# Attention and a gated FFN on one core: batch 0 with a mask product, single PSUM banks and split weight loads

## The chip, the cores and the metric

The kernel runs on one core of a Trainium2 chip. The core has a tensor engine (PE) with its weight loads (PEld), a vector engine (DVE), a scalar engine (ACT), GpSimd (POOL) and SyncE (SP), which here only issues DMAs. The metric is the device time of one execution in microseconds (us); lower is better. The median of 8 runs of the kernel before is 380.19 us (379.68 to 382.72).

## The reference

```python
B, H, S, D = 8, 8, 576, 64
scores = q @ k.T / 8
cum = cumsum(max(s, 0))                       # per head, along the sequence
scores = scores + min(-(cum[i] - cum[j]), 0)  # the bias
scores = where(j > i, -1e9, scores)           # causal mask
attn = softmax(scores) @ v
x = attn, heads side by side                  # 4608 tokens x 512
g = x @ w_gate                                # 512 x 1536
out = (silu(g) * (x @ w_val)) @ w_out         # 1536 x 512
```

All inputs are float32; the kernel computes its matrix products in bfloat16 with float32 sums.

## The kernel before

**Attention.** There are 64 heads: 8 batches of 8. Four heads make one half batch `hb` (16 of them). Q and K of a half batch are transposed into `KQ[hb % 2][r]`, where 64 partitions hold a head's channels and the other 64 hold four rows with the cumulated bias (`aug`, line 192) and zeros, so that one matmul gives score plus bias. `HL` holds these rows; it comes from `s` by a chain on DVE (lines 236 to 242). A head's scores are made transposed, keys on partitions, in four pieces (`CHUNKS`, line 56): 512 columns on the diagonal, 512, 512 and 64. ACT takes the exponential of a piece out of PSUM into `pt`, and POOL's `affine_select` sets the entries above the diagonal to zero (lines 391 and 396). `av_piece` multiplies with V and a column of ones, `av_out` divides by the sum on DVE, `x_pe` transposes the result on PE into `XT`.

**FFN.** A tile is 512 tokens; there are 9. For each of 12 blocks of 128 FFN columns, `gate_value` makes the gate product (4 matmuls of 128x512, line 626), tanh on ACT, a product on DVE, the value product (line 641) and a second product on DVE. `down_plain` or `down_seven` then multiplies with w_out.

**Order.** The program order of each engine is written out by hand. Batch 0 runs alone, in `first_batch`. After it, the FFN of tile `tt` is interleaved with the attention of batch `tt` + 1: `ffn_items` yields after each product, and `pump` advances `attn_items` in proportion. `hook` places the transposes of half batch 2 and some casts among the first items. Half batches 2 to 4 are transposed on PE (`prep_one`, `PREP_AT`), later ones through DRAM by DMA.

**PSUM.** In batch 0 it is cut into two wide tiles of two banks (1024 columns) and four single banks; `second_psum` makes eight single banks of it afterwards. In batch 0 a head's four pieces are written in pairs into a wide tile, so that ACT runs two exponentials per head, of 1024 and 576 columns. A bank is taken with `take` (the one released longest ago) and given back with `give`.

**Queues.** SP issues the loads of q, k, v and the bias rows of half batches 0, 2 and 3 (`SP4`); POOL issues the weights (`w_load`, which casts to bfloat16 on the way), the bias rows of half batch 1 (`GP4`) and the stores. Each engine runs its instructions in order, so an instruction that waits holds up all behind it. In `first_batch` the first gate and value tiles (768 columns each) are issued after head 1's scores, the second ones after heads 4 and 5, w_out after head 7. V of batch 0 is cast by POOL (three chunks, after head 2) and DVE (two chunks, after head 1). All eight heads' values come after head 6's scores:

```python
tail = {
    6: ("a0", "a1"),
    7: ("a2", "a3", "a4", "x0", "a5", "x1", "a6", "a7", "x2", "w6", "x3", "w8"),
}
```

where a is `av_piece` and `av_out` of a head, x is `x_pe` of a pair of heads and w are matmuls whose result nobody reads.

The softmax here doesn't subtract the row's maximum and nothing guards it: scores larger than these inputs give would overflow.

## Time and profile before

| | us |
|---|---|
| median of 8 runs | 380.19 |
| the profiled execution | 379.68 |
| its span | 377.9 |
| first score matmul of batch 0 | 11.21 |
| end of batch 0's last exponential | 27.03 |
| first gate product | 31.68 |
| first value product | 32.81 |

The span is the time from the first to the last instruction that the profile records; the execution's own time is 1.8 us longer. In the page, the busy share of each engine over the span is followed by 40 slices of 9.45 us, each a digit in tenths. PEclk is the share of the PE clock that was granted. The chain is followed back from the last instruction to what released each step. A row of the timeline has its start, its busy time, engine, line, operation, the tiles written and read with their shapes, and the number of instructions merged in it; in brackets stands how long the engine was idle before it and what ended that. Where one row has several shapes, the first is printed. A row of a table by stretches has the stretch, its length, each engine's busy time with its instructions, the granted clock, the mean busy share of the 16 DMA engines and GB/s. A semaphore record tells when a DMA's data landed.

### The profile page before, as it was taken

To read this page: it belongs to the slowest core of one execution; us is meant where nothing else is said; L and a number is where in the kernel's file an instruction comes from. 1 tells how busy PE (TensorE), PEld (TensorE's weight loads), DVE (VectorE), ACT (ScalarE), POOL (GpSimd) and SP (SyncE) were. 2 spreads that over 40 slices of the span, in tenths; PEclk is the share of its full clock that TensorE was granted. 3 is DMA by queue.
4 is the path that set the end of the run, shared out by engine and by line. 5 is a ranking of instruction groups with operands and counts; after the bars stand their busy time and mean duration, and the time that the engine had idled before them with its cause. 6 is when DMAs were issued, how large, how long until landed. Compare 5 with 4: busy or idle time off the path is not lost.

```text
span 377.9 us, 8674 instructions
## 1 busy us (share of the span) xinstructions
PE 361.5 (96%) x3246; PEld 229.5 (61%) x3246; DVE 290.2 (77%) x577; ACT 242.4 (64%) x459; POOL 206.5 (55%) x326
## 2 busy tenths in 40 slices
PE   3679999999999999999999999999999999999996
PEld 3566556655555546865586558655875575466465
DVE  7766787457895899769975998589958876985984
ACT  8686788677976877578766885697365523323321
POOL 7684357545374646595559556875675426224320
PEclk9899999999999999999999999999999999999999
DMA  7999999997498997498669775996323133001103
GB/s 241 198 251 262 199 260 265 343 263 169 159 170 280 214 289 202 124 291 212 166 203 287 195 161 162 231 215 144 52 71 111 24 28 128 0 2 69 43 2 111
DMA packets 100730, 64.22 MB, mean 170 GB/s; under 512 B 81889, under 2 KB 85825, under 8 KB 100689
## 3 DMA queue, kind: packets, MB, share of 16 engines
q1 hardware_dynamic: 91248, 46.15, 50.3%
q0 software_dynamic: 9440, 17.53, 17.8%
q8 instruction: 25, 0.41, 0.5%
q14 instruction: 17, 0.13, 0.1%
HBM read 37.90 MB, written 19.86 MB: 153 GB/s over the span
## 4 chain that ended last, share of the span: by engine, by line
PE 85%; DVE 6%; DMA 5%; ACT 2%; issue 1%; DVEq 0%; ACTq 0%; SPq 0%
PE bank L626 22%; PE bank L641 22%; PE bank L711 17%; PE bank L375 9%; PE bank L413 6%; PE bank L670 5%; DMA pk<-ks 3%; PE wide L375 2%; DVE pp L633 1%; ACT pt L388 1%; DVE kq L326 1%; DVE ht L649 1%; PE one L413 1%; DMA kq<-HL 1%; DMA s_sb<-in_s_dram 1%
## 5 line engine op out<-in xcount | busy, mean ns | idle before, releaser
L388 ACT ACTIVATE pt<-bank 128x512 bf16<-128x512 f32 x224 | 106.7, 507 | 26.4 <-PE bank L375 18.1
L626 PE MATMUL bank<-XT,wg 128*128 128x512 bf16 x432 | 110.9, 379 | 0.7 <-DVE pp L633 0.2
L641 PE MATMUL bank<-XT,wv 128*128 128x512 bf16 x432 | 110.9, 379 | 0.0
L631 ACT ACTIVATE th<-bank 128x512 bf16<-128x512 f32 x108 | 64.7, 599 | 58.9 <-PE bank L626 54.7
L633 DVE SCALAR_TENSOR_TENSOR pp<-th,bank 128x512 bf16<-128x512 bf16 x108 | 73.7, 683 | 23.7 <-ACT th L631 23.2
L649 DVE SCALAR_TENSOR_TENSOR ht<-pp,bank 128x512 bf16<-128x512 bf16 x108 | 74.2, 687 | 10.4
L658 POOL TENSOR_TENSOR ht<-ht 128x512 bf16<-128x512 bf16 x35 | 40.4, 1154 | 53.0 <-DVE su L656 53.0
L375 PE MATMUL bank<-kq 128*128 128x128 bf16 (+4 forms) x504 | 67.5, 240 | 0.2 <-DVE ht L649 0.2
L375 PEld LDWEIGHTS <-kq 128*128 128x128 bf16 x576 | 46.3, 99 | 33.7 <-issue 5.0
L641 PEld LDWEIGHTS <-wv 128*128 128x128 bf16 x432 | 38.3, 98 | 35.3
L626 PEld LDWEIGHTS <-wg 128*128 128x128 bf16 x432 | 38.4, 98 | 35.2 <-issue 1.1
L391 POOL TENSOR_SCALAR_AFFINE_SELECT pt<-pt 128x512 bf16<-128x512 bf16 x64 | 42.1, 657 | 30.6 <-ACT pt L388 30.0
L413 PEld LDWEIGHTS <-pt 128*128 128x128 bf16 x960 | 41.0, 98 | 16.6 <-issue 0.7
L413 PE MATMUL bank<-vt,pt 128*128 128x65 bf16 x840 | 41.8, 194 | 0.5 <-DVE ot L430 0.5
L447 POOL DMA_DIRECT2D xs<-ot x24 | 21.7, 906 | 28.2 <-DVE ot L430 28.2
L711 PEld LDWEIGHTS <-ht 128*128 128x128 bf16 x336 | 31.2, 98 | 4.3
L197 POOL DMA_DIRECT2D kq<-HL x52 | 31.3, 605 | 0.1
L430 DVE TENSOR_TENSOR ot<-bank,rc 128x320 bf16<-128x320 f32 x56 | 27.5, 492 | 1.9
L396 POOL TENSOR_SCALAR_AFFINE_SELECT pt<-pt 128x64 bf16<-128x64 bf16 x64 | 17.2, 269 | 18.5 <-ACT pt L388 18.3
L711 PEld LDWEIGHTS <-su 128*128 128x128 bf16 x252 | 23.5, 98 | 3.3
L670 PE MATMUL bank<-wo,ht 128*128 128x512 bf16 x96 | 24.7, 379 | 0.0
L776 POOL TENSOR_TENSOR ysb<-ysb 128x512 f32<-128x512 f32 x12 | 15.2, 1270 | 15.3 <-DVE ysb L770 15.3
(96 smaller groups left out, 396.1 us busy)
## 6 DMA issues: line engine op xcount, KB each, us to landing
rawk<-in_k_dram SPq DMA_DIRECT2D x15, 576.0 KB
rawq<-in_q_dram SPq DMA_DIRECT2D x15, 576.0 KB
rawv<-in_v_dram SPq DMA_DIRECT2D x32, 256.0 KB
out_dram<-ysb POOLq DMA_DIRECT2D x32, 256.0 KB, 3.7
xs<-ot POOLq DMA_DIRECT2D x24, 160.0 KB, 4.0
ks<-ck SPq DMA_DIRECT2D x11, 288.0 KB
qs<-cq SPq DMA_DIRECT2D x11, 288.0 KB
wg<-in_moe_w_gate_dram POOLq DMA_DIRECT2D x2, 768.0 KB, 12.5
```

What stands on the lines that cost most here:

```text
L375: nc.tensor.matmul(sc[:, o : o + w], T[:, 1, e * S + 128 * tj : e * S + 128 * (tj + 1)], T[:, 0, e * S + lo : e * S + hi], start=True, sto ...
L388: nc.scalar.activation(pt[:, c0 : c0 + W], sc[:, 0:W], AF.Exp, scale=0.125)
L391: nc.gpsimd.affine_select(pt[:, 1088:1600], pt[:, 1088:1600], pattern=[[0, 4], [1, 128]], compare_op=ALU.is_ge, fill=zreg, base=0, channel ...
L413: nc.tensor.matmul(av[:, bi * (D + 1) : (bi + 1) * (D + 1)], pt[:, c0 : c0 + 128], VT[b % 2][:, tj, h, :], start=(tj == 0), stop=(tj == bi),)
L626: nc.tensor.matmul(pg, WG[j][:, c, f0 : f0 + 128], xt[:, c, :], start=(c == 0), stop=(c == 3),)
L631: nc.scalar.activation(th, pg, AF.Tanh, scale=0.5)
L633: nc.vector.scalar_tensor_tensor(pp, in0=th, scalar=1.0, in1=pg, op0=ALU.add, op1=ALU.mult)
L641: nc.tensor.matmul(pv, WV[j][:, c, f0 : f0 + 128], xt[:, c, :], start=(c == 0), stop=(c == 3),)
L649: nc.vector.scalar_tensor_tensor(hp[:, 2 * k2 : 2 * k2 + 2, :].rearrange("p a n -> p (a n)"), in0=pp, scalar=0.5, in1=pv, op0=ALU.mult, op ...
L658: (nc.vector if ft == NFT - 1 else nc.gpsimd).tensor_sub(hp[:, 1:3, :], hp[:, 1:4:2, :], hp[:, 0:3:2, :])
L670: nc.tensor.matmul(py, hps[ft // 2][:, 2 * (ft % 2) + half, c0 : c0 + 128], WO[ft // WKO][:, ft % WKO, :], start=(ft == 0), stop=(ft == NF ...
L711: nc.tensor.matmul(ps, lhs(p), rhs(p), start=(first and p == 0), stop=(last and p == NP - 1), skip_group_check=True,)
```

## The change

Batch 0 is written anew, and some places in the later schedule move.

- The wide PSUM tiles are gone; eight single banks serve the whole kernel. One is set aside (`spare`) for matmuls that nobody reads (`keep_warm`): 32 at the start and twice 10 between the first transposes.
- In batch 0, POOL's selects are gone. For the two diagonal pieces a matmul of the identity with a tile `lower` (zero, or -32768 above the diagonal) is put into the bank first, and the scores are added to it. ACT runs four exponentials per head.
- The transposes of half batch 1 are split: k's after head 0, q's after head 1, with the copies of heads 4 and 5 at once and those of heads 6 and 7 after head 3.
- V of batch 0 is cast by POOL alone. The first gate and value tiles are loaded in halves of 384 columns: gate's first half ahead of the bias rows of half batch 1, value's first half after four of the five V casts, the other two after the fifth. The second tiles follow after head 3, with the casts of half batch 2 between them; w_out moves to the fifth FFN item.
- The values of heads 0 and 1 come before head 6's scores, those of 2 and 3 before head 7's, the rest behind. The last `x_pe` copies on DVE. The gate products of the first two blocks run over three of the four head pairs (`begun`) before the FFN starts, and the FFN adds the fourth.
- Seven `pt` buffers instead of eight in batch 0. Later: the second copy of a `prep_one` waits for the next item (`seconds`); the bias rows of half batch 4, some casts, splits and transposes move by a step or more.

```diff
-    PTP = {0: first, "bufs": 8}
+    PTP = {0: first, "bufs": 7}
+    lower = first.tile([128, 512], BF16)
...
-        first_psum = ExitStack()
-        psa = first_psum.enter_context(tc.tile_pool(name="psa", bufs=1, space=PSUM))
-        bank = {}
-        for i in range(2):
-            bank["w", i] = psa.tile([128, 1024], FP32, name=f"wide{i}")
-        for i in range(4):
-            bank["s", i] = psa.tile([128, 512], FP32, name=f"one{i}")
-        released = {key: i - 8 for i, key in enumerate(bank)}
+        psb = ctx.enter_context(tc.tile_pool(name="psb", bufs=1, space=PSUM))
+        bank = {i: psb.tile([128, 512], FP32, name=f"bank{i}") for i in range(8)}
+        released = {i: i - 8 for i in bank}
...
+        nc.gpsimd.memset(lower, 0.0)
+        nc.gpsimd.affine_select(
+            lower, lower, pattern=[[0, 4], [1, 128]],
+            compare_op=ALU.is_ge, fill=nc.gpsimd.to_reg(MASKED), base=0, channel_multiplier=-1,
+        )
...
-        init_vt(0)
-        init_vt(1)
...
+            masked = bh < H
             if ci == 0:
                 pts[bh] = PTP[0].tile(
-                [128, PTW], BF16, tag="pt", bufs=PTP["bufs"], name="pt"
-            )
+                    [128, PTW], BF16, tag="pt", bufs=PTP["bufs"], name="pt"
+                )
             pt = pts[bh]
             r, e = divmod(hh, 2)
             T = KQ[hb % 2][r]
-            if pair:
-                if ci % 2 == 0:
-                    bs = take("w")
-                    scs[bh] = bs
-                else:
-                    bs = scs[bh]
-                base = (512, 0, 0, 512)[ci]
-            else:
-                bs = take()
-                base = 0
-            o = base
+            bs = take()
             n = sum(hi - lo for _, lo, hi in CHUNKS[ci])
-            sc = view(bs, 1024 if pair else 512)
+            sc = view(bs, n)
+            masked_here = masked and ci in (0, 3)
+            if masked_here:
+                nc.tensor.matmul(
+                    sc, ident, lower[:, 0:n], start=True, stop=False, skip_group_check=True
+                )
+            o = 0
             for (tj, lo, hi) in CHUNKS[ci]:
                 w = hi - lo
                 nc.tensor.matmul(
                     sc[:, o : o + w],
                     T[:, 1, e * S + 128 * tj : e * S + 128 * (tj + 1)],
                     T[:, 0, e * S + lo : e * S + hi],
-                    start=True,
+                    start=not masked_here,
                     stop=True,
+                    skip_group_check=masked_here,
                 )
                 o += w
-            if not pair or ci % 2 == 1:
-                if pair:
-                    c0, W = ((576, 1024), (0, 576))[ci // 2]
-                else:
-                    c0, W = CHUNK_PT[ci], n
-                nc.scalar.activation(pt[:, c0 : c0 + W], sc[:, 0:W], AF.Exp, scale=0.125)
-                give(bs)
-            if ci == (1 if pair else 0):
+            c0 = CHUNK_PT[ci]
+            nc.scalar.activation(pt[:, c0 : c0 + n], sc, AF.Exp, scale=0.125)
+            give(bs)
+            if masked:
+                return
+            if ci == 0:
...
-                first = 1 if hb < NPE + 2 else 0
+                first = 1 if hb < NPE + 3 else 0
...
-                if (step, ci) == ((1, 1) if late else (0, 2)):
+                if (step, ci) == ((1, 3) if late else (0, 2)):
                     cast_one(hb, "k", nc.scalar)
-                if (step, ci) == ((2, 1) if late else (1, 2)):
+                if (step, ci) == ((2, 2) if late else (1, 2)):
                     cast_one(hb, "q", nc.scalar)
...
+        V4_AT = {(0, 0): 0, (1, 0): 1, (2, 0): 2, (3, 0): 3, (3, 2): 4}
+
         def side_v(h, step, ci):
             bn = h // 2 + 1
-            if 2 <= bn < B and h % 2 == 1 and (step, ci) in V_AT:
-                cast_v(bn, V_AT[step, ci], nc.scalar if bn > 2 else nc.gpsimd)
+            at = V4_AT if bn == 4 else V_AT
+            if 2 <= bn < B and h % 2 == 1 and (step, ci) in at:
+                cast_v(bn, at[step, ci], nc.scalar if bn > 2 else nc.gpsimd)
...
-            for r in range(2):
-                pe_out(hb, nm, g, r, nc.scalar if nm == "k" else nc.vector)
+            eng = nc.scalar if nm == "k" else nc.vector
+            pe_out(hb, nm, g, 0, eng)
+            seconds.append(lambda: pe_out(hb, nm, g, 1, eng))
...
-            2: {(0, 3): 0, (1, 3): 1, (2, 1): 2, (2, 3): 3},
+            2: {(1, 1): 0, (1, 3): 1, (2, 1): 2, (2, 3): 3},
...
-                    if step == 0 and 3 < h + 1 < NPE:
+                    if step == 2 and 3 < h + 1 < NPE:
...
+        begun = {}
+
+        def products(kind, ft, xt, cs=range(4)):
+            j, f0 = divmod(ft * 128, WCH)
+            w = (WG if kind == "g" else WV)[j]
+            if (kind, ft) in begun:
+                bs, c0 = begun.pop((kind, ft))
+                cs = range(c0, 4)
+            else:
+                bs = take()
+            for c in cs:
+                nc.tensor.matmul(
+                    view(bs, TT), w[:, c, f0 : f0 + 128], xt[:, c, :],
+                    start=(c == 0), stop=(c == 3),
+                )
+            if cs[-1] < 3:
+                begun[kind, ft] = bs, cs[-1] + 1
+            return bs
...
+        spare = take()
+
+        def keep_warm(n):
+            for _ in range(n):
+                nc.tensor.matmul(view(spare, 128), ident, ident, start=True, stop=True)
+
+        def row_half(nm, r, eng):
+            for g in range(2):
+                pe_transpose_half(0, nm, g, r)
+            for g in range(2):
+                pe_out(0, nm, g, r, eng)
+
+        def half_batch(nm):
+            for g in range(2):
+                pe_transpose(1, nm, g)
+                pe_out(1, nm, g, 0, nc.vector)
+
+        def scores(h):
+            for ci in range(4):
+                score_piece(h, ci)
+
+        def values(*hs):
+            for h in hs:
+                av_piece(h, range(NCH))
+                av_out(h)
+
+        keep_warm(32)
         cast_half(0, "k", 0, nc.scalar)
         cast_half(0, "q", 0, nc.scalar)
         aug(0, SP4)
         load_v(0, range(5))
         load_qk(2)
+        row_half("k", 0, nc.scalar)
+        row_half("q", 0, nc.vector)
+        cast_half(0, "k", 1, nc.scalar)
+        cast_half(0, "q", 1, nc.gpsimd)
+        w_load("g", 0, 0)
+        aug(1, GP4)
+        init_vt(0)
+        keep_warm(10)
+        row_half("k", 1, nc.scalar)
+        row_half("q", 1, nc.vector)
+        keep_warm(10)
+        cast_one(1, "k", nc.vector)
+        cast_one(1, "q", nc.vector)
+        for c in range(4):
+            cast_v(0, c, nc.gpsimd)
+        w_load("v", 0, 0)
+        cast_v(0, 4, nc.gpsimd)
+        w_load("g", 0, 1)
+        w_load("v", 0, 1)
+        scores(0)
+        half_batch("k")
+        scores(1)
+        half_batch("q")
+        scores(2)
+        scores(3)
         for nm in ("k", "q"):
             for g in range(2):
-                pe_transpose_half(0, nm, g, 0)
-        pe_out(0, "k", 0, 0, nc.scalar)
-        pe_out(0, "k", 1, 0, nc.scalar)
-        pe_out(0, "q", 0, 0, nc.vector)
-        pe_out(0, "q", 1, 0, nc.vector)
-        cast_half(0, "k", 1, nc.scalar)
-        cast_half(0, "q", 1, nc.gpsimd)
-        aug(1, GP4)
-        for nm, eng in (("k", nc.scalar), ("q", nc.vector)):
-            for g in range(2):
-                pe_transpose_half(0, nm, g, 1)
-                pe_out(0, nm, g, 1, eng)
-        cast_one(1, "k", nc.vector)
-        cast_one(1, "q", nc.vector)
-
-        def keep_warm(n):
-            bs = take()
-            for _ in range(n):
-                nc.tensor.matmul(
-                    view(bs, 128), ident, ident, start=True, stop=True
-                )
-            give(bs)
-
-        def first_batch():
-            wq = {1: (("g", 0), ("v", 0)), 4: (("g", 1),), 5: (("v", 1),)}
-            tail = {
-                6: ("a0", "a1"),
-                7: ("a2", "a3", "a4", "x0", "a5", "x1", "a6", "a7", "x2", "w6", "x3", "w8"),
-            }
-            for h in range(H):
-                for ci in range(4):
-                    score_piece(h, ci)
-                for w in wq.get(h, ()):
-                    w_load(*w)
-                if h == 1:
-                    order = [(nm, g) for g in range(2) for nm in ("k", "q")]
-                    for nm, g in order:
-                        pe_transpose(1, nm, g)
-                    for r in range(2):
-                        for nm, g in order:
-                            pe_out(1, nm, g, r, nc.vector)
-                    for c in range(3, 5):
-                        cast_v(0, c, nc.vector)
-                if h == 2:
-                    for c in range(3):
-                        cast_v(0, c, nc.gpsimd)
-                if h == 3:
-                    aug(2, SP4)
-                if h == 7:
-                    aug(3, SP4)
-                    load_qk(3)
-                    load_v(1, range(5))
-                    load_qk(4)
-                    cast_one(2, "k", nc.gpsimd)
-                    cast_one(2, "q", nc.gpsimd)
-                    load_qk(5)
-                    w_load("o", 0)
-                    w_load("o", 1)
-                for what in tail.get(h, ()):
-                    i = int(what[1:])
-                    if what[0] == "a":
-                        av_piece(i, range(NCH))
-                        av_out(i)
-                    elif what[0] == "x":
-                        x_pe(i, nc.scalar)
-                    else:
-                        keep_warm(i)
-
-        first_batch()
-        second_psum()
+                pe_out(1, nm, g, 1, nc.vector)
+        aug(2, SP4)
+        w_load("g", 1)
+        cast_one(2, "k", nc.gpsimd)
+        cast_one(2, "q", nc.gpsimd)
+        w_load("v", 1)
+        scores(4)
+        scores(5)
+        values(0, 1)
+        scores(6)
+        values(2, 3)
+        scores(7)
+        aug(3, SP4)
+        load_qk(3)
+        load_v(1, range(5))
+        load_qk(4)
+        load_qk(5)
+        init_vt(1)
+        values(4, 5)
+        x_pe(0, nc.scalar)
+        values(6, 7)
+        x_pe(1, nc.scalar)
+        x_pe(2, nc.scalar)
+        x_pe(3, nc.vector)
+        for ft in range(2):
+            products("g", ft, XT[:, :, 0:TT], range(3))
+        give(spare)
...
+            5: [lambda: w_load("o", 0), lambda: w_load("o", 1)],
...
+                while seconds:
+                    seconds.pop(0)()
```

## The prediction

> **What bounds the kernel now.** First the page: PE's row and its slices, then the chain.
>
> ```profile
> PE 361.5 (96%) x3246; PEld 229.5 (61%) x3246; DVE 290.2 (77%) x577; ACT 242.4 (64%) x459; POOL 206.5 (55%) x326
> ...
> PE   3679999999999999999999999999999999999996
> ...
> PEclk9899999999999999999999999999999999999999
> DMA  7999999997498997498669775996323133001103
> ...
> PE 85%; DVE 6%; DMA 5%; ACT 2%; issue 1%; DVEq 0%; ACTq 0%; SPq 0%
> ```
>
> PE is full from the fourth slice to the end; only the first three (28 us) have room. The DMA digits say that the engines moving data are full up to about 94 us. In the chain of waits nearly every 128x512 group of four takes 0.86 us, 0.216 each. Setting each matmul's start-to-start time against its columns at that rate leaves 3.5 us of PE stall after 31.68 us, 2.0 of it near 41, 49 and 136 us. So the end is **the time of the first gate product, plus a fixed load of PE, plus stalls**. The timeline shows what sets that start:
>
> ```profile
> 11.21 0.86 PE L375 MATMUL wide<-kq 128*128 128x128 bf16 x9 [1.22 <-DMA kq<-HL]
> 16.90 4.99 ACT L388 ACTIVATE pt<-wide 128x1024 bf16<-128x1024 f32 x6 [1.38 <-PE wide L375]
> 27.14 0.24 POOL L396 TENSOR_SCALAR_AFFINE_SELECT pt<-pt 128x64 bf16<-128x64 bf16 x1
> 29.87 0.49 DVE L430 TENSOR_TENSOR ot<-one,rc 128x320 bf16<-128x320 f32 x1
> 30.99 0.64 ACT L468 COPY XT<-one 128x576 bf16<-128x576 bf16 x1 [0.52 <-PE one L463]
> 31.68 1.02 PE L626 MATMUL bank<-XT,wg 128*128 128x512 bf16 x4 [0.17 <-ACT XT L468]
> ```
>
> Head 0 waits for its bias rows, ACT's exponentials then run to 27.03 (two gaps, three with the start), POOL masks the last head, and values, normalisation, transpose and copy follow one another to 31.68.
>
> **The change, part by part.**
>
> *Start to 11.2 us.* The bias rows' path (s, DVE's scan, HL, SP's DMAs) has the same instructions. Warm-up matmuls fill PE while it waits: 32 x 0.107 = 3.4 us from 1.4 us end before the first cast at 5.35. Nothing. The ten after q's first half may push k's second half by 0.5 us; ACT has 1.6 us free before 11.86. Nothing. POOL's mask tile costs about 0.5 (a 64x512 memset took 0.52) plus 0.63 (a 128x512 select), against 1.8 us of v-tile memsets moved away; POOL idled 1.3 us there anyway.
>
> *Exponentials.* Wide: heads start 1.715 apart in steady state. Single banks: the full head at 39.41 has its three 512s 0.48 apart, and a 64 adds 0.11: 1.55 per head. First exponential at 11.6 (after 512 columns, not 1024) instead of 11.86; eight heads end at 11.6 + 8 x 1.55 = 24.0. Only three banks stay free while half_batch holds four: refilling one costs PE 0.44 plus about 0.4 of latency, against 0.6 to 1.0 of exponentials beside it; I take 0.4 us off: **24.4** if nothing else stops ACT (before 27.03).
>
> *Mask by a product.* 0.216 + 0.03 us of PE per head, 2.0 in all, beside 0.67 of scores: 0.92 under ACT's 1.55, so hidden; 2.0 us if PE were the bound. POOL loses 8 x (0.655 + 0.259) = 7.3 us. On the path it removes the last POOL step, 0.35 us.
>
> *V casts, all on POOL.* The semaphore records put V's five chunks at 14.4, 15.5, 16.7, 18.1 and 19.2. POOL's casts were 0.56 apart; c3 ends at 18.9, the load of the first value half is issued (0.8), c4 ends at **20.4**. Behind this wait on POOL: both later half loads, then g1 and batch 1's casts. PE wants these values after head 5's scores, near 20, and heads 6 and 7 stand behind them in PE's order.
>
> *The gate half beside the bias rows.* Its issue (0.8) comes ahead of aug(1) on POOL, so those rows land by 15 to 16 instead of 13.9; head 4 wants them at 17.8. Here a rule speaks against the change: the Trainium skill, "DMA: Bandwidth & Descriptors", section "Issuing engines are not separate DMA queues", says that DMAs of all engines run on the same 16 and interleave. The rows:
>
> ```profile
> 8.00:10.00 2.00, 1.88 (x18) 1.71 (x18) 1.38 (x3) 1.17 (x3) 1.76 (x3) 1.00 0.97 383
> 10.00:12.00 2.00, 0.79 (x9) 0.65 (x10) 1.97 (x4) 0.39 (x2) 1.44 (x3) 1.00 0.23 60
> 12.00:22.00 10.00, 6.75 (x63) 5.46 (x61) 7.35 (x12) 7.68 (x10) 7.18 (x14) 0.83 1.14 260
> 22.00:30.00 8.00, 7.24 (x162) 6.34 (x161) 4.66 (x16) 6.14 (x9) 6.92 (x13) 1.00 1.16 212
> ```
>
> Last but one column: DMA share. There is a hole at 10 to 12. aug(1), issued at 8.90 on the same queue, had its first packet 1.34 us later. If the half (512 packets, each half of a 135 ns packet, on 16 engines: 2.2 us) starts at 10.4, most lies in the hole, and V comes 0.3 later or less. By the rule, with the whole half interleaved with V, V lands 1.9 later: c4 at 22.0 and the start 1.6 later. I take the hole, since these rows show the engines free when the half arrives, and keep 22.0 for the range.
>
> *Clock.* The skill's "TensorE: Matmul & The Clock Gate", section "What's actually happening", says that an idle window of about 3.4 us halves the clock. The page's 8 in PEclk is that: 0.5 from 13.0 to 16.4 in the clock record, with batch 0's 18 transposes 0.107 apart. The section "PE-mode transpose" says that transposes don't count as busy, which would leave the clock low in the new order too: 0.9 us more for the same 18. By the warm-up matmuls it stays full. It falls beside ACT's work either way, so on the path I take 0.2.
>
> *The tail.* With c4 at 20.4, PE finishes the two heads' values at about 21.1, head 6's exponentials run 21.6 to 23.1, values 2 and 3, head 7's exponentials 23.6 to 25.1, its values end at 25.9. DVE's eight normalisations at 0.67 from 20.8 give 26.2 or, behind the last values, 26.7. Transpose to 27.2, and six of the gate products (1.3 us) start at once while DVE copies (0.46). Start at 27.2 to 28.8 (c4 at 22.0); with 0.4 for banks I take **28.2, or 3.5 earlier**. The price if the six didn't cover the copy is 0.6.
>
> *After the start.* Total PE work is unchanged. `seconds` takes one of two 0.8 us copies out of DVE's burst at 40 to 49 us: 0 to 1.0 of stall back, I take 0.3; the stall at 136 I leave. w_out's loads move behind the value tile (POOL 1.7 us more at about +5; they landed at 46.7 and 51.7, first wanted at 61.7). aug for heads 16 to 19 moves two heads later, to about 62: rows under load landed 5.4 to 6.8 after issue, wanted near 71. Casts of k5 and q5 go later on ACT, V4's earlier, PREP_AT and `first` by one step: each moves work of 0.5 to 1.2 us among free spaces of ACT and DVE; nothing, or 0.3 either way.
>
> *What is late next* is DMA. Batch 1's V shares the engines with weights:
>
> ```profile
> 53.86 1.17 POOL L183 CAST vt<-rawv 128x512 bf16<-128x512 f32 x2 [0.50 <-DMA rawv<-in_v_dram]
> 55.39 0.35 PE L413 MATMUL bank<-vt,pt 128*128 128x65 bf16 x6
> ```
>
> PE first uses it at 55.39. c2 was cast by 53.37 and c4 by 55.03, wanted at about 56.6 (head 0's scores began on its own bias row at 11.16 while head 1's landed at 11.5, so waits are by region): slack 1.5 to 2.0. The filled hole brings all later transfers 1.0 to 1.9 forward, so PE may come 2.8 to 3.3 earlier before it waits here. That cuts 3.5 + 0.3 to **3.0**. Against the profiled execution: span 377.9 - 3.0 = 374.9, time 379.68 - 3.0 = 376.7; the median shown is 0.5 above that execution, so 380.19 - 3.0 = 377.2.
>
> **Rivals.**
> *V of batch 1 takes the gain.* If the half's packets find no hole, or smaller packets cost more, later transfers come at best 0 to 0.5 earlier, and PE stops at batch 1's values with 0.5 to 1.5 left in place of 3.0: 379.2. For it: DMA share 1.14 from 30 to 54 and that 0.50 wait. Against it: the slack above.
> *The V cast of batch 0 sets the start.* c4 at 23 or later (V delayed and POOL waiting on each chunk): each us goes straight to the start, about 30.5 to 31.5; 379.8.
> *Slower: the first value half.* It is issued only after c3, at 19.8 to 21.4, against 16.6 for the whole tile before. Before, the gate tile took 4.7 us to its first packet and 10.6 to land, the value tile 13.6. Half the bytes with nothing ahead: 4.7 + 2.9 = 7.6, landing at 27.4 to 29.0; the first value product comes at about 29.7, so it decides nothing up to 30. With the old 13.6 from 20.8 it lands at 34.4, while the old kernel ran that product at 32.8: 1.6 slower, 381.8. It decides beyond 32.8.
> *The change doesn't do what it says*: a mask product kept out of the cover of ACT shows as at most 2.0 us of PE and turns 3.0 into 1.0; this is inside the range.
>
> **How the numbers follow.** Main case 0.58 (375.8 to 378.6), V of batch 1 0.20, V cast 0.07, slower 0.15. No change that a measurement can tell is 0.3%, 1.14 us, so 379.05 to 381.33. Faster: 0.57 of the main case and 0.06 of the first rival, 0.63; slower: 0.15 and a little for unknown stalls, 0.16; same 0.21. The range takes the main case, both rivals of little gain, and part of the slower one: 375.6 to 381.0.
>
> **What would show it.** The first gate product at 27 to 29; exponentials 1.55 apart per head up to head 5, then a wait of PE for V's cast of at most 1 us; DMA share at 10 to 12 well above 0.23; no POOL select before batch 1; PEclk without an 8; PE stall after the start still under 4 us. Wrong if the first value product waits for its weights, if heads are over 1.7 apart, or if PE stops at batch 1's values by more than 1 us.

## The result, and the profile after

The changed kernel takes 383.69 us (median of 11 runs, 381.13 to 386.75). The kernel before, run beside it, takes 380.48 us (32 runs, 378.92 to 382.72). The ratio is 1.0088, 95% interval [1.0066, 1.0109]: **0.9% slower**, where 0.8% faster was forecast. The profiled execution took 383.09 us (before: 379.68), its span is 381.4 us (377.9).

The page of the changed kernel: PE's busy row, PE's slices, the clock, the DMA slices, and the shares of the chain.

```profile
PE 366.3 (96%) x3300; PEld 232.0 (61%) x3300; DVE 291.1 (76%) x576; ACT 242.7 (64%) x474; POOL 204.2 (54%) x316
...
PE   7889989989999999999999999999999999999995
...
PEclk9999999999999999999999999999999999999999
DMA  7999999999577986698869765995123013002103
...
PE 73%; DMA 12%; DVE 6%; SPq 4%; POOL 2%; issue 1%; ACT 1%; DVEq 0%; ACTq 0%
```

PE is fuller at the left edge (first three slices 7, 8, 8 instead of 3, 6, 7), but those at 48 to 57 and at 76 to 86 us are 8. The clock row has no 8 any more. In the chain, DMA rose from 5% to 12%, SyncE's queue (SPq) from 0% to 4%, and PE fell from 85% to 73%: the end now hangs more often on data that had not come. The start, in the timeline (rows of ACT, PE and POOL):

```profile
11.58 10.18 ACT L368 ACTIVATE pt<-bank 128x512 bf16<-128x512 f32 x24 [1.59 <-PE bank L358]
...
20.99 0.31 PE L395 MATMUL bank<-vt,pt 128*128 128x65 bf16 x5 [0.79 <-POOL vt L168]
...
21.66 0.62 POOL L168 CAST vt<-rawv 64x512 bf16<-64x512 f32 x1
...
22.34 0.65 PE L395 MATMUL bank<-vt,pt 128*128 128x65 bf16 x16 [1.04 <-POOL vt L168]
...
23.47 1.69 ACT L368 ACTIVATE pt<-bank 128x512 bf16<-128x512 f32 x4 [1.70 <-PE bank L358]
...
29.57 1.69 PE L618 MATMUL bank<-XT,wg 128*128 128x512 bf16 x7
```

Six heads of exponentials run through in 10.18 us, 1.70 each. Then PE waits for the last two casts of V. Head 6's scores stand behind those values in PE's order, so ACT idles 1.70 us, and the last exponential ends at 27.06, where it ended before (27.03). What is earlier is the part behind it: the first gate product comes at 29.57, 2.1 us before the old 31.68. The same four stretches that the prediction showed of before:

```profile
8.00:10.00 2.00, 1.67 (x25) 1.39 (x25) 1.24 (x3) 1.44 (x3) 1.66 (x3) 1.00 0.94 368
10.00:12.00 2.00, 1.48 (x22) 1.01 (x20) 1.97 (x4) 0.42 (x1) 2.00 (x4) 1.00 0.83 88
12.00:22.00 10.00, 7.42 (x89) 5.22 (x86) 6.25 (x9) 9.52 (x24) 5.08 (x9) 1.00 1.21 251
22.00:30.00 8.00, 7.43 (x150) 6.07 (x150) 5.44 (x17) 5.20 (x11) 7.81 (x11) 1.00 1.23 199
```

The hole at 10 to 12 us is filled by share (0.83 instead of 0.23), but hardly by bytes: 88 GB/s instead of 60. At 22 to 30 us a higher share (1.23 instead of 1.16) moves less (199 GB/s instead of 212). Adding up the packets that ended by a given time (both queues):

| MB landed by | 16 us | 24 us | 28 us | 50 us | 60 us |
|---|---|---|---|---|---|
| before | 3.45 | 5.56 | 6.41 | 11.35 | 14.53 |
| after | 3.52 | 5.49 | 6.27 | 11.17 | 14.01 |

PE is 2.1 us ahead; the data are not ahead at all. Most of them were not asked for sooner either. SP's rows, the first three of before, the last three of after:

```profile
16.47 9.96 SPq L197 DMA_DIRECT2D kq<-HL  x8
26.53 0.39 SPq L155 DMA_DIRECT2D rawk<-in_k_dram  x1
27.53 24.13 SPq L172 DMA_DIRECT2D rawv<-in_v_dram  x5
...
18.26 8.17 SPq L183 DMA_DIRECT2D kq<-HL  x8
26.52 0.39 SPq L140 DMA_DIRECT2D rawk<-in_k_dram  x1
27.60 24.92 SPq L157 DMA_DIRECT2D rawv<-in_v_dram  x5
```

In SP's order, half batch 3's q and k and batch 1's V stand behind eight bias rows. The last four of these go into `KQ[1]`, which the scores of heads 4 to 7 still read. Head 7's scores came no earlier than before, so its row was issued at 25.81 in both kernels, and V at 27.60 (before 27.53). Of POOL's loads only the first gate half (8.94 instead of 15.82) and w_out (28.22 instead of 29.51) were issued earlier; the rest of the first two tiles (20.88 to 22.97 instead of 15.82 and 16.62) and the second tiles (23.70 and 26.61 instead of 22.37 and 23.91) were later.

The lead of PE over the data shows at two places further on, both in the timeline: PE at batch 1's values with the POOL cast that they wait for, and then tile 1's gate product at 80 us with what DVE does ahead of it:

```profile
53.36 0.32 PE L395 MATMUL bank<-vt,pt 128*128 128x65 bf16 x5
...
54.39 0.62 POOL L168 CAST vt<-rawv 128x512 bf16<-128x512 f32 x1 [1.08 <-DMA rawv<-in_v_dram]
...
55.06 0.19 PE L395 MATMUL bank<-vt,pt 128*128 128x65 bf16 x1 [1.38 <-POOL vt L168]
...
79.16 0.81 PE L618 MATMUL bank<-XT,wg 128*128 128x512 bf16 x3
...
80.76 0.45 DVE L273 COPY kq<-pk 64x1152 bf16<-64x1152 bf16 x1 [3.86 <-DMA pk<-ks]
81.14 0.44 DVE L452 COPY XT<-bank 128x576 bf16<-128x576 bf16 x1
81.63 0.38 PE L618 MATMUL bank<-XT,wg 128*128 128x512 bf16 x1 [1.66 <-DVE XT L452]
```

At 53 us the V chunk is late, POOL casts it as soon as it lands, and PE stands for 1.38 us. At 80 us the DVE copy of half batch 5's transposed k waits 3.86 us for a DMA. The copy to XT is queued behind it, and PE's gate product needs XT. By the prediction's own measure (start to start of each matmul against its columns) the stalls after the first gate product are 8.75 us, where they were 3.55 (time lost to a halved clock counts as a stall here); PE's own work after it is 338.9 us in both kernels. The 5.2 us more are 1.74 at 53 to 57, 1.82 at 80, 0.8 more at 132 to 139, 0.8 at 217 and 0.1 elsewhere. So 2.1 us are gained at the start and 5.2 lost later, about 3.1 in all; the two profiled executions are 3.4 apart.

### The profile page after: what moved, and what is told of

Its sections match the earlier page's. It is cut to its first block, busy times and chain, and to the rows that moved or that the text cites. A ratio compares the mean times of both kernels' runs of the same rounds, so it can differ in the third digit from the quotient of the medians.

```text
span 381.4 us, 8792 instructions
## 1 busy us (share of the span) xinstructions
PE 366.3 (96%) x3300; PEld 232.0 (61%) x3300; DVE 291.1 (76%) x576; ACT 242.7 (64%) x474; POOL 204.2 (54%) x316
## 4 chain that ended last, share of the span: by engine, by line
PE 73%; DMA 12%; DVE 6%; SPq 4%; POOL 2%; issue 1%; ACT 1%; DVEq 0%; ACTq 0%
PE bank L618 40%; PE bank L707 17%; DMA rawv<-in_v_dram 8%; PE bank L358 8%; PE bank L395 6%; SPq L157 3%; PE bank L666 3%; DMA pk<-ks 2%; DMA ks<-ck 2%; DVE pp L634 1%; DVE kq L273 1%; DVE ht L645 1%; DMA s_sb<-in_s_dram 1%; SPq L183 1%; POOL wv L331 1%
## 5 line engine op out<-in xcount | busy, mean ns | idle before, releaser
L368 ACT ACTIVATE pt<-bank 128x512 bf16<-128x512 f32 (+1 forms) x256 | 120.2, 509 | 30.7 <-PE bank L358 21.3
L358 PE MATMUL bank<-kq 128*128 128x128 bf16 (+4 forms) x576 | 75.1, 240 | 0.8 <-DMA kq<-HL 0.5
L618 PEld LDWEIGHTS <-wg 128*128 128x128 bf16 x432 | 38.5, 98 | 37.4 <-issue 3.1
L395 PE MATMUL bank<-vt,pt 128*128 128x65 bf16 x960 | 46.8, 194 | 4.1 <-POOL vt L168 3.2
L373 POOL TENSOR_SCALAR_AFFINE_SELECT pt<-pt 128x512 bf16<-128x512 bf16 x56 | 36.1, 644 | 23.7 <-ACT pt L368 23.1
L412 DVE TENSOR_TENSOR ot<-bank,rc 128x320 bf16<-128x320 f32 x64 | 31.5, 492 | 2.2
L183 POOL DMA_DIRECT2D kq<-HL x52 | 32.3, 624 | 0.0
L378 POOL TENSOR_SCALAR_AFFINE_SELECT pt<-pt 128x64 bf16<-128x64 bf16 x56 | 15.3, 272 | 18.8 <-ACT pt L368 18.7
L411 DVE RECIPROCAL rc<-bank 128x5 f32<-128x5 f32 x64 | 12.1, 189 | 16.7 <-PE bank L395 16.4
```

The lines of the kernel that those rows point to most:

```text
L183: engs[hh].dma_start(KQ[hb % 2][r][r0 : r0 + 4, :, e * S : (e + 1) * S], HL[bh : bh + 1, :, :, :],)
L358: nc.tensor.matmul(sc[:, o : o + w], T[:, 1, e * S + 128 * tj : e * S + 128 * (tj + 1)], T[:, 0, e * S + lo : e * S + hi], start=not maske ...
L368: nc.scalar.activation(pt[:, c0 : c0 + n], sc, AF.Exp, scale=0.125)
L373: nc.gpsimd.affine_select(pt[:, 1088:1600], pt[:, 1088:1600], pattern=[[0, 4], [1, 128]], compare_op=ALU.is_ge, fill=zreg, base=0, channel ...
L395: nc.tensor.matmul(av[:, bi * (D + 1) : (bi + 1) * (D + 1)], pt[:, c0 : c0 + 128], VT[b % 2][:, tj, h, :], start=(tj == 0), stop=(tj == bi),)
L618: nc.tensor.matmul(view(bs, TT), w[:, c, f0 : f0 + 128], xt[:, c, :], start=(c == 0), stop=(c == 3),)
```

## The experiments

**What was asked.** The first theory: the data of the first 80 us are the bound that holds the new order back. Rivals: the place of the weight loads, the later edits, or PE's new order itself. The kernel before ran beside each one on the same chip; times are medians. The ratio is worked out from the single runs and is not the quotient of the two medians: where the runs fall into two groups, as in e14, it differs from that.

| kernel | us | before | ratio, 95% | first gate product | stall after it |
|---|---|---|---|---|---|
| e1_whole | 383.18 | 379.83 | 1.0087 [1.0065, 1.0109] | 28.30 | 10.5 |
| e2_casts | 382.08 | 379.83 | 1.0067 [1.0048, 1.0086] | 29.90 | 7.3 |
| e3_late_new | 380.12 | 379.83 | 1.0017 [1.0001, 1.0033] | 31.77 | 3.2 |
| e4_late_old | 382.30 | 379.83 | 1.0065 [1.0048, 1.0082] | 31.29 | 6.6 |
| e5_mid | 381.14 | 379.98 | 1.0028 [1.0013, 1.0044] | 28.06 | 9.8 |
| e6_wo | 382.96 | 379.98 | 1.0094 [1.0059, 1.0129] | 29.51 | 8.4 |
| e7_mid_wo_casts | 381.75 | 379.98 | 1.0041 [1.0019, 1.0062] | 28.03 | 10.2 |
| e8_halves | 380.30 | 379.98 | 1.0013 [1.0000, 1.0027] | 29.47 | 5.7 |
| e9_before_less | 379.84 | 379.73 | 0.9994 [0.9979, 1.0009] | 31.33 | 3.5 |
| e10_after_less | 379.50 | 379.73 | 0.9992 [0.9971, 1.0013] | 31.23 | 5.5 |
| e11_after_less_casts | 379.76 | 379.73 | 1.0002 [0.9983, 1.0021] | 29.64 | 5.3 |
| e12_mid_casts | 382.04 | 379.73 | 1.0065 [1.0035, 1.0095] | 33.59 | 3.7 |
| e13_before_warm | 380.78 | 380.14 | 1.0022 [1.0008, 1.0037] | 29.91 | 5.5 |
| e14_before_less_warm | 378.55 | 380.14 | 0.9978 [0.9958, 0.9997] | 34.74 | 3.6 |
| e15_after_fill | 383.02 | 380.14 | 1.0105 [1.0068, 1.0143] | 29.40 | 7.8 |
| e16_warm_wo | 380.05 | 380.14 | 1.0010 [0.9991, 1.0028] | 29.88 | 5.6 |

The last two columns are of the one profiled execution, and the last one has in it what a halved clock costs; in e9 to e12, 39 matmul records are missing from the trace, and 8.5 us of apparent gap (39 times 0.22) are taken off.

### The place and the halves of the weight loads: e1, e5, e8

```diff
 e1_whole (from the changed kernel)
-        w_load("g", 0, 0)
         aug(1, GP4)
...
-        w_load("v", 0, 0)
         cast_v(0, 4, nc.gpsimd)
-        w_load("g", 0, 1)
-        w_load("v", 0, 1)
+        w_load("g", 0)
+        w_load("v", 0)
 e5_mid (from the changed kernel): both whole tiles between the first and the second cast_v
 e8_halves (from the kernel before)
-            wq = {1: (("g", 0), ("v", 0)), ...
+            wq = {1: (("g", 0, 0), ("v", 0, 0), ("g", 0, 1), ("v", 0, 1)), ...
```

> The changed kernel with the first gate and value tiles loaded whole, both behind the fifth V cast, none beside the bias rows. Theory 'transfers' (the four half loads take more DMA time than two whole ones, and the first of them holds up V of batch 0): the five V casts end near 20.4 us instead of 22.3, PE's wait of 1.4 us for batch 1's V (near 53.5 us) shrinks below 0.5, and the time falls by 1 to 2 us against the changed kernel (383.7), even if the first value product waits up to 1 us for its whole tile. Theory 'late moves' (the casts and splits moved later make the loss): the time stays within 0.5 us of 383.7 and the stall near 80 us stays.

> The changed kernel with the first gate and value tiles whole, issued between the first and the second V cast (near 15 us, as early as before), nothing beside the bias rows. Theory 'order of transfers' (the half beside the bias rows pushes V back by 1.6 us, and a weight load issued to an idle queue near 21 us spends its first us almost without bytes): V casts end near 20.4, the value tile lands near 30 to 31, the first gate product comes by 28.5, batch 1's V is cast by 55.2 instead of 56.3; the time falls by 1.5 to 2.5 us, to about 381.5. Theory 'late moves alone': no change beyond 0.7 us, the stall near 80 us stays.

> The kernel before with its first gate and value tiles loaded as four halves in the same place, nothing else. The halves' 768-byte packets took 79 ns against 135 for 1536 bytes, so 2.5 us per half instead of 2.15: the four halves land 1.4 us later than the two tiles did (30.2), near 31.6. The first value product is at 32.8, so the start is unchanged and the time within 0.7 us of before, unless batch 1's V, 1.5 to 2.0 us ahead of PE, comes late too.

Without the early half (e1) the first gate product comes 1.3 us sooner, at 28.30, and V of batch 0 is cast by 20.05 instead of 22.29: the early half did delay V. But value weights issued that late hold PE for 3.8 us at 30, the clock record then has half from 32.31 to 39.13, and the time is the same as the change's. PE, so delayed, no longer waits at 53 or at 80 us. With the loads earlier (e5) the gate product comes at 28.06, the value weights hold PE for 1.7 us, V of batch 1 for 2.3, k of half batch 5 for 2.2: 381.1 us, the best of the new orders with all loads, and still slower than before. The time is the one forecast, but not by its way: batch 1's V was cast by 56.9, not 55.2. (The profiled execution was the slowest of its eight, 382.73.)

e8 gave more than it was made for. Its first gate product came at 29.47, 2.2 us before that of the kernel before, with the same work of PE, ACT and DVE in the same order. Its row, and the first of its waits at batch 1's values:

```profile
29.47 0.81 PE L626 MATMUL bank<-XT,wg 128*128 128x512 bf16 x3 [0.17 <-ACT XT L468]
...
53.93 0.19 PE L413 MATMUL bank<-vt,pt 128*128 128x65 bf16 x1 [0.44 <-POOL vt L183]
```

Its execution took 379.73 us and the other 379.68. PE stood 1.54 us at batch 1's values and 0.68 at 59.6, where the kernel before had no such wait: **a start 2.2 us earlier was given back in full, in the old order too.** Why it started earlier is taken up with e13.

### The later edits: e2, e3, e4, e12

```diff
 e2_casts (from the changed kernel): the casts of k5 and q5 back
-                if (step, ci) == ((1, 3) if late else (0, 2)):
+                if (step, ci) == ((1, 1) if late else (0, 2)):
...
-                if (step, ci) == ((2, 2) if late else (1, 2)):
+                if (step, ci) == ((2, 1) if late else (1, 2)):
 e4_late_old: all of the later edits back (these casts, first, V4_AT, seconds, PREP_AT, aug)
 e3_late_new: the kernel before with all of these later edits
 e12_mid_casts: e5_mid with the casts of e2_casts
```

> The changed kernel with the two casts of half batch 5 on ACT put back to their old pieces. Theory 'late moves': the stall of 1.8 us near 80 us, where DVE waits for the transposed k ahead of a copy to XT, goes, and the time falls by 1.3 to 1.8 us. Theory 'transfers': the transfer of the transposed k is late because all DMA is late, the stall falls by less than 0.7 us, and so does the time.

> The kernel before with only the later edits of the change (second copies deferred, bias rows of half batch 4 two heads later, casts, splits, transposes moved), batch 0 as before. Theory 'late moves': slower than before by 1.5 to 3 us. Theory 'transfers': within 0.7 us of before, since nothing there delays a transfer of the first 50 us.

> The changed kernel with all those later edits put back, batch 0 as in the change. Theory 'late moves': about 380 us or a little less, as the first gate product still comes 2 us earlier. Theory 'transfers': 382 to 384, with the wait for batch 1's V near 53 us unchanged.

> A complete kernel: the changed one with the first gate and value tiles whole, issued between the first and the second cast of V (as in e5_mid), and the casts of half batch 5 at their old places (as in e2_casts). e5_mid measured 381.1 with 2.2 us of wait at 80 us and 2.3 at 53 to 57. Theory: the wait at 80 us goes, a part of it (0.7 to 1.0) comes back as a wait for V or k near 61: 379.5 to 380.5, no better than the kernel before by anything that can be told. Rival: the casts are worth their whole 2.2: 378.9.

With the casts back the wait at 80 us is gone; a wait of 1.04 at 62 comes in, and the ratio falls from 1.0088 to 1.0067, with intervals that overlap. Taking all later edits back (e4) gives no more than that. In the old order the same edits cost 0.2% (e3), at the edge of what can be told. So what the later casts cost is not shown: each of the two differences is some 0.2%, and one of them is inside the noise. e12 missed both of its forecasts, 382.04 against 379.5 to 380.5: in its profiled execution the last V chunk was cast at 23.74 instead of 20.78, with the same instructions as e5 up to there. The stretches of that execution show a second price of such a wait (last but two: the granted clock):

```profile
18.00:22.00 4.00, 2.47 (x36) 1.90 (x36) 0.43 (x1) 3.80 (x10) 0.37 (x1) 1.00 1.14 196
22.00:26.00 4.00, 2.21 (x24) 1.70 (x24) 1.37 (x4) 0.28 (x1) 1.30 (x2) 0.56 1.12 275
26.00:30.00 4.00, 4.00 (x60) 3.33 (x59) 1.38 (x4) 2.18 (x6) 1.14 (x1) 0.58 1.12 272
```

PE waited 3.3 us at 20.5 to 23.8 and was clocked at half from 22.5 to 29.3, 6.8 us; with the wait, this put the first gate product at 33.59.

### w_out behind V of batch 1: e6, e7

```diff
-            5: [lambda: w_load("o", 0), lambda: w_load("o", 1)],
             6: [lambda: cast_one(3, "k", nc.gpsimd), lambda: cast_one(3, "q", nc.gpsimd)],
+            12: [lambda: w_load("o", 0), lambda: w_load("o", 1)],
```

(e6_wo from the changed kernel; e7_mid_wo_casts with e5's loads and e2's casts too.)

> The changed kernel with w_out's two loads issued at the twelfth FFN item instead of the fifth, where POOL ran them at 28 us because nothing held it. Theory 'order of transfers': batch 1's V lands some 5 us earlier, PE's wait of 1.7 us near 53 to 56 us goes, w_out lands by 58 and is wanted after 61; the time falls by 1.5 us and more. Theory 'late moves alone': the wait near 53 goes, but PE only reaches the stall near 80 us earlier and waits longer there, so the time falls by less than 0.5 us.

> Both of these edits, and the two casts of half batch 5 at their old pieces. If the order of transfers and the two casts make the whole loss: 377 to 379, faster than the kernel before (380). If something else in the new batch 0 costs time: 380 or more.

V of batch 1 is cast by 51.9 instead of 56.3 and PE no longer waits for it. It waits for w_out instead, as PE's rows in e6 show:

```profile
61.32 0.60 PE L666 MATMUL bank<-wo,ht 128*128 128x512 bf16 x2
...
64.17 0.65 PE L666 MATMUL bank<-wo,ht 128*128 128x512 bf16 x2 [2.26 <-DMA wo<-in_moe_w_out_dram]
```

The clock record has half for the 3.4 us from 64.58 on. The wait at 80 us is gone, against the second theory, but the time is unchanged (1.0094). e7 is alike: gate product at 28.03, a wait of 2.4 for w_out at 60.5, half the clock from 63.07 to 66.49, and 381.75 us, as in its second forecast (380 or more). In these two the queue order only chose which data were late.

### Fewer data: e9, e10, e11

```diff
-    WV = [const.tile([128, 4, WCH], BF16, name=f"wv{j}") for j in range(NWCH)]
+    WV = [const.tile([128, 4, WCH], BF16, name="wv0")] * NWCH
...
-        w_load("v", 1)
```

> The kernel before without the load of the second value tile (the second half of the value columns uses the first tile again; 1.5 MB less to read before 45 us). Theory (the transfers of the first 80 us are the bound that holds the new order back; the old order just meets them): PE's stalls after the start were 3.55 us in the profile, of which at most 0.7 to 1.0 belong to late data, so 379.0 to 379.9 where the kernel before has 380.0; V of batch 1 is cast by 49 to 51 instead of 55. Rival (PE's own order is the bound, data are incidental): within 0.3 of the kernel before.

> The changed kernel without the load of the second value tile. Theory: the waits for V of batch 1 (1.7 us at 53 to 56) go, the wait for the transposed k of half batch 5 at 80 us (1.8) stays since casts set it: 383.2 - 1.7 to 2.2 = 381.0 to 381.5. Rival: the new order costs PE time by itself, so 382.8 to 383.7, as with all loads.

> The changed kernel without the load of the second value tile and with the casts of half batch 5 at their old places. Theory: both waits go; the 2.1 us gained at the start are kept but for 0.5 to 1.0 (the waits at 132 to 139 and 217 us): 378.3 to 379.5, faster than the kernel before and by 0.5 or more faster than the kernel before with the same load left out. Rival: the value of the casts alone, 382.1, and slower than both.

This one load, 1.5 MB to read, is worth nothing to the kernel before (379.84 beside 379.73) and **some 4 us to the changed one**: 379.50 instead of 383.69, or by the ratios 1.0088 to 0.9992, 3.6 us. That is as much as its whole loss, and more than either forecast of e10 allowed. V of batch 1 is cast by 53.6 without a wait of PE (in e11, which starts at 29.64, by 52.3), and the wait at 80 us is gone as well, against the expectation; so the old places of the casts are then worth nothing (e11, 379.76). PE in e11, at batch 1's values and at 80 us, with no idle time in front:

```profile
53.42 0.35 PE L395 MATMUL bank<-vt,pt 128*128 128x65 bf16 x6
...
54.47 0.90 PE L395 MATMUL bank<-vt,pt 128*128 128x65 bf16 x24
...
79.81 1.03 PE L618 MATMUL bank<-XT,wg 128*128 128x512 bf16 x4
```

But e11 was expected at 378.3 to 379.5, faster than e9, and is not: in its execution PE starts 1.7 us before e9's and stalls 1.8 us longer.

### The clock and the order of batch 0: e13, e14, e15, e16

```diff
 e13_before_warm (from the kernel before; e14_before_less_warm: e9_before_less with the same)
+        keep_warm(32, "w")
         cast_half(0, "k", 0, nc.scalar)
...
         aug(1, GP4)
+        keep_warm(10, "w")
...
+        keep_warm(10, "w")
         cast_one(1, "k", nc.vector)
 e15_after_fill (from the changed kernel)
         scores(5)
+        keep_warm(24)
         values(0, 1)
 e16_warm_wo: e13_before_warm, w_load("o", 1) moved from first_batch to the 9th FFN item
```

> The kernel before with the warm-up matmuls of the changed one alone (32 at the start, twice 10 between the first transposes), all else as it was. Theory (the clock, not the order of batch 0, gives most of the earlier start, and late data take the gain): full clock from about 7 us on, eight heads of exponentials as close as in e8_halves, first gate product at 29.0 to 30.0 instead of 31.68; V of batch 1 then holds PE for 1.2 to 2.0 us near 54; time 379.5 to 380.4, no better than before. Rival: PE is the bound after the start, so the start is kept: 377.8 to 378.5.

> The same with the load of the second value tile left out. Theory: with 1.5 MB less to read PE is the bound, the earlier start is kept: 377.5 to 378.3, that is 1.5 to 2.2 below the kernel before with only the load left out (379.8). If something else than data sets the end (the bursts of DVE at 129 to 139 us), 379.3 to 379.9.

> The changed kernel with 24 further matmuls that nobody reads between head 5's scores and the values of heads 0 and 1, where PE waits for V's casts. Theory (that idle stretch halves the clock for 3.4 or 6.8 us in some executions, and then the first gate product comes at 31.3 or later): the clock stays full, gate at 29.5 to 30.0, the spread of the times gets smaller and the median falls by 0.3 to 1.0 to 382.7 to 383.4; the waits for data at 53 and 80 us stay. Rival: no change of the median (383.7) nor of the spread.

> A complete kernel, the candidate: the kernel before with the warm-up matmuls and with the second half of w_out loaded only at the ninth FFN item. Theory: V of batch 1 comes 1 to 2 us sooner, so part of the start is kept, and w_out's second half (first wanted after its first half, from 63 us) is in time: 378.3 to 379.5. Rival: the same bytes are wanted by 61 us, w_out comes late by what V gains, as in e6_wo: 380 to 381.

The warm-up matmuls alone give the old order a first gate product at 29.91 (e16: 29.88), within 0.4 of the changed kernel's 29.57. The exponentials of e13's first seven heads are two nearly unbroken blocks; below them, its first gate product:

```profile
11.51 3.28 ACT L388 ACTIVATE pt<-wide 128x1024 bf16<-128x1024 f32 x4 [1.46 <-PE wide L375]
...
15.02 8.42 ACT L388 ACTIVATE pt<-wide 128x1024 bf16<-128x1024 f32 x10 [0.23 <-PE wide L375]
...
29.91 1.02 PE L626 MATMUL bank<-XT,wg 128*128 128x512 bf16 x4 [0.17 <-ACT XT L468]
```

In the prediction's rows of the kernel before, the third head began at 16.90 after a gap of 1.38; here it begins at 15.02. The clock records agree: full from 4.6 us on in e13, from 9.5 in e8 (the early one), only from 16.7, 15.0 and, after a dip, 16.4 in e3, e9 and the kernel before. So the **earlier start is the clock's work**; mask product, single banks, value order and the three-pair products add 0.3 us between them in these executions, since the wait for V's casts takes back what they save. Where V is not held up so, in e1, e5 and e7, the first gate product comes at 28.0 to 28.3, 1.6 to 1.9 before e13's.

And the start so gained is worth nothing while all loads are there: 380.78 beside 380.14, by the ratio 0.1 to 0.4% slower. The place of the wait was not the expected one. PE stands for 1.50 us at 38.5, for the cast of half batch 3's k, whose load SP issued at 30.04 instead of 26.53; for 0.41 at V of batch 1; for 0.68 at 59.8, for another cast of k. Why SP came to this load so late in e13 is not shown; in e8 it was issued at 26.35, and the start was given back all the same. Leaving out the one load is worth 0.44% to this order, 1.7 us (e14's ratio of 0.9978 against e13's 1.0022 on the same chip, with intervals apart), and with the cold start it was worth nothing (e9). e14's interval, [0.9958, 0.9997], is the only one here below 1; 12 of its 22 runs lie between 377.5 and 378.75, and its median of 378.55 is just outside the 377.5 to 378.3 of the theory. So the gain at the start is real, PE can keep some of it, and the data of the first 60 us do not let it. How much is not settled: e14 is ahead of e9 by 1.3 us in the medians and by 0.6 in the ratios, on different chips and with intervals that overlap. e14's profiled execution was one of its late ones (382.75 us: last V cast at 25.07, clock halved, gate at 34.74).

e15 fills the idle stretch as meant: gate at 29.40, clock full. But the median (383.02, ratio 1.0105) is not better than the change's 1.0088 by anything that can be told, and the spread stays (382.07 to 387.14). Its waits at 53 and 80 us were 1.0 and 0.5, less than the change's. The halved clock occurs after a wait in eight of the eighteen profiles (before, e1, e4, e6, e7, e10, e12, e14), but not in the changed kernel's own, and that it is a part of that kernel's median is not shown. e16 brought V of batch 1 no sooner (56.27), for 380.05; that is in its rival's range but not by its mechanism: w_out was on time, and PE waited for V (1.4 us) and k (0.7) as before. **No version beat the kernel before with all its data loaded.**

**What stays open.** With less data the new order (379.50) stands about 1 us behind the old one with a warm clock (378.55), on different chips; by the ratios (0.9992 and 0.9978) the intervals overlap, so the difference is not shown. In the profiles its stalls are 5.3 to 5.5 against 3.5 to 3.6 us, but not at one place: in e11 1.4 of them lie at 129 to 132 us, where the release of a bank by DVE comes late behind a burst of work on w_out (so too in e15, 1.8), in e10 1.8 at 251 to 256, where DVE's copy of k waited 2.3 us for its DMA. Which edit moves DVE there was not tried. Why the data come no sooner is only in part known: most loads are issued no earlier, and from 12 us on the DMA share is over 1 in both kernels. Which of the two holds was not separated; in e1 batch 1's V was issued 1.6 us earlier (26.00) and cast 1.0 later (57.3), with the weights issued later.

## Why the prediction was wrong

- **"The end is the time of the first gate product, plus a fixed load of PE, plus stalls"**: right as an account (338.9 us of PE work after the start in both). The failing steps are the two variable terms.
- **"The filled hole brings all later transfers 1.0 to 1.9 forward", "cuts 3.5 + 0.3 to 3.0"**: this is the step that turned the sign. No byte came forward (11.17 MB by 50 us instead of 11.35): the hole at 10 to 12 us took in only 28 GB/s more, or 0.06 MB, and V's loads were issued no earlier (27.60 instead of 27.53); V of batch 1 was cast by 56.3 instead of 55.0 while PE came 2.1 earlier, so the slack of 1.5 to 2.0 was overrun and 1.74 us of wait came in. e8 and e13 show that an earlier start is given back in the old order too, e10 and e14 that this ends with 1.5 MB less. The rival "V of batch 1 takes the gain" had the mechanism and too small a price: it let V take at most the gain. Of the 5.2 us of new stalls V has 1.74; the rest comes later, and with 1.5 MB less it is gone in the time too (e10). Two of the prediction's own signs of being wrong were there: PE stopped at batch 1's values by more than 1 us, and three of the five head distances were 1.77 to 1.81.
- **"I take the hole ... c4 ends at 20.4"**: wrong, 22.29. The rejected number, 22.0 by the section "Issuing engines are not separate DMA queues" of the Trainium skill's "DMA: Bandwidth & Descriptors", was right within 0.3: the half landed at 14.74 instead of inside the hole, V's chunks 1.6 to 2.2 later than before. The hole was there in the row, but all traffic together came to 88 GB/s while it lasted. Without that half V is cast by 20.05 (e1).
- **"By the warm-up matmuls it stays full", "on the path I take 0.2"**: the first half is right, the size is not. Warm-up alone moves the first gate product by 1.8 us (e13), nearly the whole gain. The term was small because the low clock was placed beside ACT's work, where it costs nothing; the third head's exponential, at 16.90 before and 15.02 in e13, shows that ACT waited for PE there.
- **"Transposes don't count as busy"**, **"an idle window of about 3.4 us halves the clock"**: the first is not so here, and the second asks for too much. In the kernel before PE did nothing but transposes from 6.17 to 9.58, and the clock was full from 9.58 on (in e8 the same, from 9.50). Its dip at 13.0 came after a window, 9.58 to 12.99, in which PE waited for bias rows and exponentials and was idle for 2.08 of the 3.41 us, not for all of them.
- **"1.55 per head"**, **"24.4"**: the exponentials at 1.55 per head were 1.70 with the waits for banks, and ended with the stall at 27.06 instead of 24.4. The start was 29.57, not 28.2, and outside its 27.2 to 28.8.
- **"Half of a 135 ns packet"**: 768-byte packets took 91 ns on average (median 79). The four halves took 11.7 us of the 16 engines' time, two whole tiles 8.6. Since e1 and e5, with whole tiles, had data no sooner, this is a mis-sized term and not the cause.
- **"Casts of k5 and q5 go later on ACT ...: nothing, or 0.3 either way"**: wrong with all loads: the wait of 1.82 at 80 us, gone in e2, where the time is some 0.2% less, with overlapping intervals. It was right where data were early (e10 and e11 alike). The later cast was priced by ACT's free space, not by the DMA that begins with it and that DVE waited for (3.86 us).
- **"seconds ... I take 0.3"**: nothing; PE's stalls at 36 to 52 us are about 1.1 us in both kernels (0.8 in e3, with the old batch 0). The wait at 136 did not stay as it was, with 0.8 more there and at 217.
- **"w_out's loads move ... +5"**: they were issued at 28.2, 1.3 earlier than before, because POOL came to them without a wait. w_out was on time; but it ran beside batch 1's V, which e6, with w_out later, has 4.4 us sooner.
- **"Mask by a product ... hidden"**, **"the first value half"** as a rival: right. No POOL select is left in batch 0, and ACT is busy for 9.52 of the 10 us from 12 to 22; the first value half landed at 26.26 and nobody waited for it.

## What to carry to other kernels

Before shortening a stage, compare what the engine would ask for with the bytes that have landed by then: here, with the DMA slices at 9, a start 2.2 us earlier only moved the wait (e8), and a run without one load, for each of the two orders, showed it. Look also at when the loads are issued: a faster stage gains nothing from a load that stands in its queue behind an instruction that comes no earlier. A start that differs between two executions of the same instructions is a free experiment: look at the granted clock first, and whether the end moved with the start. Price a late load by the first consumer that stands behind its waiting instruction (PE at 80 us, behind DVE's copy), not by the free space of the engine that starts it.

## What the runs showed of the hardware

PE in the kernel before, ahead of the first full clock at 9.58: all of it transposes.

```profile
5.40 1.17 PE L311 MATMUL one<-ident,ck 128*64 128x128 bf16 x9 [5.40 <-ACT ck L264]
6.36 1.17 PE L311 MATMUL one<-ident,cq 128*64 128x128 bf16 x9
8.12 1.17 PE L311 MATMUL one<-ident,ck 128*64 128x128 bf16 x9 [0.59 <-ACT ck L264]
9.08 0.91 PE L311 MATMUL one<-ident,cq 128*64 128x128 bf16 x9
```

- The granted clock changes only at the edges of windows of 3.41 us, whose phase differs between executions (the first full window began at 4.4 to 7.5 us in the profiles with warm-up). How long PE was idle within one window went with the clock of the next one. In all 18 profiles, up to the kernel's last 10 us and by the profile's modelled busy time, windows at full clock with up to 1.66 us of idle time kept it; those with 1.86 (e10), 1.87 (e4) and from 2.02 on (before, e1, e6, e7, e12, e14) halved it for 3.4 us or, where PE idled another 1.3 to 1.6 us in the halved window, for 6.8 (e1, e12, e14). One window with 2.00 (e5, at 80.5) kept it.
- So the same waits can cost nothing or a halved clock. The two waits for V's casts, 0.7 to 0.8 and 1.04 us, fall into one window in e4 and e10 (19.5 to 22.9 and 19.6 to 23.0), and an edge parts them in after (20.7) and e11 (21.4).
- The first POOL load of the changed kernel was slow at first: from 11 to 12 us its packets kept the 16 engines busy (share 1.02, with those begun before) and moved 61 KB, a third of the 187 KB of the next us. A high DMA share is not a high rate.
- While these weight packets began, SP's queue nearly stopped: at 11 to 13 us its packets took 0.02 of the engines' time, and the last bias row of half batch 0 landed at 14.96, 5.1 us after its issue. Before, it took 0.40 of their time then, and that row landed at 12.46, 2.2 us after its issue.
